# A four-tap shift convolution moved from VectorE products to TensorE matmuls with diagonal tap matrices, fed by transposing DMAs, in a kernel of two state-space layers

## The chip, the cores and the metric

The kernel runs on one core of one Trainium2 chip. The metric is the device time of one execution in microseconds. Three runs of the kernel before gave 431.73 us in the median, from 428.91 to 433.8. The profile is of one execution, with a span of 431.1 us from the first to the last instruction.

## The reference, cut to what matters

Two layers are computed side by side and their outputs are joined along the last axis. Layer A (S = 2048 rows, D = 1024 channels) starts with the four-tap convolution that the change is about, multiplies by v, applies a long convolution over the whole sequence by means of Fourier transforms, and multiplies by q:

```python
k_pad = jnp.pad(k, ((0, 0), (ks - 1, 0), (0, 0)))
k_shift = jnp.zeros_like(k)
for t in range(ks):                       # ks = 4
    k_shift = k_shift + k_pad[:, t:t + S, :] * shift_k[:, ks - 1 - t][None, None, :]
kv = k_shift * v
...
y = irfft(rfft(kv, padded to 2S) * rfft(ssm_k, padded to 2S))[:S]
y = y + kv * ssm_D
return q * y
```

Layer B is a diagonal complex recurrence: `Bu = x @ B_bar^T`, `h = Lam_bar * h + Bu[t]` along the 2048 rows, `y = 2 * real(h @ C^T) + x * Dskip`. Inputs and output are bf16.

## The kernel before, in words

The sequence of layer A is written as row = 16 n1 + n2, with n1 from 0 to 127 on the partitions and n2 from 0 to 15 as a loop. One tile is thus 128 rows, 16 apart, by 1024 channels. The Fourier transform is factored along this split, in three stages with DRAM scratch between them:

- A1. For each n2: the shift convolution and the product with v give kv (`a1_kv_ops`, L397 to L418), two 128-point transforms by matmul with F1t go to PSUM and are evicted by ScalarE (`a1_kv_mm`, L427 and L428) and stored to Ys_kv. Beside it, ssm_k is loaded in quarters (`a1h_load`), transposed on TensorE (`a1h_T`, L451), transformed (`a1h_mm`, L474) and stored to Ys_h.
- A2. For each of 32 groups g: second transforms of both (L508), the product of the spectra (L519, L521 on VectorE) and the first inverse transform (L532, L533), stored to Vs.
- A3. For each n2: the last inverse transform (L562, L563) and the product with q.

Layer B runs all the way beside these in 16 chunks of 128 rows: u = x @ B_bar^T (`b_u`, L274, 128 matmuls of 128 columns a chunk), rotation and scans on VectorE (`b_rot_ops`, L292 to L331; the scans are L305 and L308), and the output matmuls (`b_y`, L345 and L350). A prologue prepares tables and transposes B (`bt_prep`, L596 to L605); C is loaded and transposed (`ct_prep`, L618) during A1.

In the kernel before, one step n2 of the convolution uses four row tiles of k, krows[n2] to krows[n2-3]. Since neighbouring rows lie in neighbouring n2, a tap is another tile, not another partition; only for n2 < 3 is a tile needed that is shifted by one partition, with zero in the first row (`a1_load_k`, L380 to L389, with two loads for it). The taps, one per channel, are broadcast over all partitions as wbc (L374 to L378: a broadcast DMA, then two ScalarE copies). VectorE then makes four products and three sums (L406, L409, L410) and the product with v (L414), each 128x1024 in bf16.

The order of the work comes from two places. The kernel sorts closures into ticks: `at(t, kind, fn)` puts one under a tick, and each tick is issued as misc work, then TensorE work of B and A interleaved, then VectorE work of B and A interleaved. One chunk of B takes eight ticks, one n2 of A1 two (`A1_STEP`), A1 ending near tick 34. The Tile framework then orders the instructions of each engine at build time and sets semaphores; every engine and every DMA queue works its list in order. Loads go out on the queue of SP (`dma`, L85), stores on that of GpSimd (`dmas_`, L88). A tile pool with bufs = n makes the tile n allocations later wait until the earlier one is released. The pools that matter here: psa (PSUM, 3 buffers, shared by all matmuls of A), krow (6), vt (3), acc (2), hk (2 buffers of a full quarter, two times 128x2048), bn (3, for loads of B and C), and u and xT, whose depths follow U_BUFS = 5 (L245, L246). `u_tick` (L638 to L665) spreads the work of `b_u` over the ticks, at 1.5 units a tick until tick 40 and 0.7 after, no further ahead than U_BUFS chunks allow.

Of the kernel before, what the change touches and what calls it, by code (L numbers as in the profile page):

```python
# [13 lines left out]
ALU = mybir.AluOpType  # L14
F32 = mybir.dt.float32
BF16 = mybir.dt.bfloat16
# [4 lines left out]
N1, N2, NFFT = 256, 16, 4096  # L21
# [40 lines left out]
def full_kernel(ctx, tc, A_q, A_k, A_v, A_shift_k, A_ssm_k, A_ssm_D, B_x, B_Lre, B_Lim, B_Bre, B_Bim,  # L62
                B_Cre, B_Cim, B_log_dt, B_Dskip, out, cfg=None):
    cfg = dict(cfg or {})
    nc = tc.nc
    P = 128
    S, D = A_q.shape[-2], A_q.shape[-1]
# [3 lines left out]
    ND = D // P  # L71
# [3 lines left out]
    NH = D // 512  # L75
# [8 lines left out]
    def dma(out_, in_):  # L84
        return nc.sync.dma_start(out_, in_)  # L85
# [9 lines left out]
    ps_a = ctx.enter_context(tc.tile_pool(name="ps_a", bufs=3, space=PSUM))  # L95

    ident = const.tile([P, P], BF16, name="ident")
# [144 lines left out]
    hpool = ctx.enter_context(tc.tile_pool(name="b_h", bufs=2))  # L242
    ypool = ctx.enter_context(tc.tile_pool(name="b_y", bufs=2))
    state = {}
    U_BUFS = cfg.get("u_bufs", 5)  # L245
    XT_BUFS = U_BUFS + 2  # L246

    def b_load_x(i):
# [16 lines left out]
    def b_u(i, j, c):  # L265
        xT = state[("xT", i)]
        if j == 0 and c == 0:
            state[("u", i)] = upool.tile([P, 2, NJ, T], BF16, name="u", bufs=U_BUFS)
        jl = j % 2
# [94 lines left out]
    pools = {}  # L364
    kr = k.rearrange("(n s) d -> n s d", s=N2)
# [3 lines left out]
    krows = {}  # L369
    A1 = {}  # L370

    def a1_setup():
        a1 = pools["a1"]
        A1["wbc"] = a1.tile([P, 4, D], BF16, name="wbc", bufs=1)  # L374
        wraw = a1.tile([P, 2, S], BF16, name="hk", bufs=2)
        for hf in range(2):
            nc.gpsimd.dma_start(wraw[:, hf, :], A_shift_k[hf * (D // 2):(hf + 1) * (D // 2), :].rearrange("d j -> (d j)").partition_broadcast(P))
            nc.scalar.copy(A1["wbc"][:, :, hf * (D // 2):(hf + 1) * (D // 2)], wraw[:, hf, :].rearrange("p (d j) -> p j d", j=4))  # L378

    def a1_load_k(n2):  # L380
        a1 = pools["a1"]
        t_ = a1.tile([P, D], BF16, name="krow", bufs=6)
        if n2 >= 0:
            dma(t_[:], kr[:, n2, :])
        else:
            nc.gpsimd.memset(t_[0:1, :], 0.0)
            dma(t_[1:113, :], kr[0:112, N2 + n2, :])
            dma(t_[113:P, :], kr[112:P - 1, N2 + n2, :])
        krows[n2] = t_  # L389

    def a1_load_v(n2):
        a1 = pools["a1"]
        vt = a1.tile([P, D], BF16, name="vt", bufs=3)
        dma(vt[:], vr_[:, n2, :])
        A1[("vt", n2)] = vt

    def a1_kv_ops(n2):  # L397
        ops = []
        st = {}
        wbc = A1["wbc"]  # L400

        def o0():
            a1 = pools["a1"]
            st["acc"] = a1.tile([P, D], BF16, name="acc", bufs=2)
            st["m"] = a1.tile([P, D], BF16, name="m", bufs=1)
            nc.vector.tensor_mul(st["acc"][:], krows[n2 - 3][:], wbc[:, 3, :])  # L406
        ops.append(o0)
        for jj in (2, 1, 0):
            ops.append(lambda jj=jj: nc.vector.tensor_mul(st["m"][:], krows[n2 - jj][:], wbc[:, jj, :]))  # L409
            ops.append(lambda: nc.vector.tensor_add(st["acc"][:], st["acc"][:], st["m"][:]))  # L410

        def o7():
            vt = A1.pop(("vt", n2))
            nc.vector.tensor_mul(st["acc"][:], st["acc"][:], vt[:])  # L414
            A1[("kv", n2)] = st["acc"]
            krows.pop(n2 - 3)
        ops.append(o7)
        return ops  # L418

    def a1_kv_mm(n2, c, dh):  # L420
        a1 = pools["a1"]
# [12 lines left out]

    def a1h_load(qd):
        a1 = pools["a1"]
        hk = a1.tile([P, 2, S], BF16, name="hk", bufs=2)
        for t_ in range(2):
            dma(hk[:, t_, :], A_ssm_k[(2 * qd + t_) * P:(2 * qd + t_ + 1) * P, :])
        A1[("hk", qd)] = hk  # L440

    def a1h_T(qd, n2g, eng):
        a1 = pools["a1"]
        hk = A1[("hk", qd)]
        hkv = hk[:].rearrange("p t (n s) -> p t s n", s=N2)
        hT = a1.tile([P, 4, DQ], BF16, name="hT", bufs=2)
        A1[("hT", qd, n2g)] = hT
        pt = ps_t.tile([P, 4, 2, P], BF16, name="pt")
        for n2l in range(4):
            for t_ in range(2):  # L450
                nc.tensor.transpose(pt[:, n2l, t_, :], hkv[:, t_, 4 * n2g + n2l, :], ident[:])  # L451
        dst = hT[:, :, :]
        src = pt[:].rearrange("p a b c -> p a (b c)")
        if eng == "v":
            nc.vector.tensor_copy(dst, src)
        else:
            nc.scalar.copy(dst, src)
        if n2g == 0:
            dsd = a1.tile([1, DQ], BF16, name="dsd", bufs=1)
            nc.gpsimd.dma_start(dsd[:], A_ssm_D.rearrange("(o d) -> o d", o=1)[:, qd * DQ:(qd + 1) * DQ])  # L460
            nc.vector.tensor_add(hT[0:1, 0, :], hT[0:1, 0, :], dsd[:])
        if n2g == 3:
            A1.pop(("hk", qd))
# [52 lines left out]
    def a2_prod(g, which):  # L516
        x16, ha, hb = gstate[g]
        if which == 0:
            nc.vector.tensor_mul(ha[:], x16[:], ha[:])  # L519
        else:  # L520
            nc.vector.tensor_mul(hb[:], x16[:], hb[:])  # L521
# [112 lines left out]
    def at(t, kind, fn):  # L634
        assert t < NT, (t, NT)
        ev.setdefault(max(t, -1), {}).setdefault(kind, []).append(fn)
# [8 lines left out]
    for t in range(8 * NCH):  # L645
        rate = U_RATE1 if t < U_T_DRAIN else U_RATE2
        quota += rate
        while n_done < 8 * NCH:
            i_, j_ = divmod(n_done, 8)
            must = n_done < t + 8 + 2  # L650
            buf_ok = (i_ - U_BUFS) * 8 + 8 <= t - 1
            if i_ - U_BUFS < 0:
                buf_ok = True
# [40 lines left out]
    if DO_A:  # L694
        a1_last = 0
        for n2 in range(N2):
            b = A1_T0 + int(n2 * A1_STEP)
            if n2 >= 1:
                at(b - 4, "misc", lambda n2=n2: (a1_load_k(n2), a1_load_v(n2)))
            kvops = {}  # L700
            at(b, "misc", lambda n2=n2, kvops=kvops: kvops.update({"l": a1_kv_ops(n2)}))
            for oi in range(8):
                at(b + (0 if oi < 4 else 1), "dve_a", lambda oi=oi, kvops=kvops: kvops["l"][oi]())
            for bi_, (c, dh) in enumerate([(0, 0), (0, 1), (1, 0), (1, 1)]):
                at(b + 2 + bi_ // 2, "pe_a", lambda n2=n2, c=c, dh=dh: a1_kv_mm(n2, c, dh))
            a1_last = max(a1_last, b + 3)
        for qd in range(NQ):
            for n2g in range(4):
                b = A1H_T0 + (4 * qd + n2g) * A1H_STEP
                if n2g == 0 and qd + 1 < NQ:  # L710
                    at(b, "misc", lambda qd=qd: a1h_load(qd + 1))
                at(b, "pe_a", lambda qd=qd, n2g=n2g: a1h_T(qd, n2g, "s"))
                for n2l in range(4):
                    at(b + 1 + n2l // 2, "pe_a", lambda qd=qd, n2=4 * n2g + n2l: a1h_mm(qd, n2))
                a1_last = max(a1_last, b + 2)
        A2_T0 = cfg.get("a2_t0", a1_last + 6)
        assert A2_T0 - 4 > a1_last

        def switch_a2():
            cms["a1"].__exit__(None, None, None)  # L720
            cms["a2"] = tc.tile_pool(name="a2", bufs=2)
            pools["a2"] = cms["a2"].__enter__()
            a2_load(0)
            a2_load(1)
        at(A2_T0 - 4, "misc", switch_a2)
        a2_last = 0
        for g in range(NG):
            b = A2_T0 + g * A2_STEP
            if g % GC == 0 and g // GC + 2 < NG // GC:
                at(b, "misc", lambda g=g: a2_load(g // GC + 2))  # L730
            for bi_, (src, dh) in enumerate([(0, 0), (0, 1), (1, 0), (1, 1)]):
                at(b + bi_ // 2, "pe_a", lambda g=g, src=src, dh=dh: a2_s2(g, src, dh))
            at(b + 3, "dve_a", lambda g=g: a2_prod(g, 0))
            at(b + 3, "dve_a", lambda g=g: a2_prod(g, 1))
            for dh in range(NH):
                at(b + 5, "pe_a", lambda g=g, dh=dh: a2_sa(g, dh))
            a2_last = max(a2_last, b + 5)
        A3_T0 = cfg.get("a3_t0", a2_last + 8)

        def switch_a3():  # L740
            cms["a2"].__exit__(None, None, None)
            cms["a3"] = tc.tile_pool(name="a3", bufs=2)
            pools["a3"] = cms["a3"].__enter__()
        at(a2_last + 1, "misc", switch_a3)
        for n2 in range(N2):
            b = A3_T0 + int(n2 * A3_STEP)
            at(max(b - 6, a2_last + 2), "misc", lambda n2=n2: a3_load(n2))
            for dh in range(NH):
                at(b, "pe_a", lambda n2=n2, dh=dh: a3_mm(n2, dh))
            at(b + 2, "dve_a", lambda n2=n2: a3_fin(n2))  # L750
# [94 lines left out]
```

## Time and profile before

| what | value |
|---|---|
| median of three runs | 431.73 us (428.91 to 433.8) |
| span of the profiled execution | 431.1 us |
| TensorE busy | 380.7 us (88%), 3713 matmuls |
| VectorE busy | 350.7 us (81%), 642 instructions |
| ScalarE busy | 303.6 us (70%), 531 instructions |
| GpSimd busy | 130.2 us (30%) |
| DMA | 102.23 MB, mean 237 GB/s |
| mean granted TensorE clock | 0.974 |
| convolution on VectorE (L406, L409, L410, L414) | 10.9 + 32.4 + 32.3 + 10.8 us |
| tap copies on ScalarE (L378) | 4.1 us |
| loads of k | 22 DMAs, 4.6 us to landing for the full ones |

How to read it: the busy time of an engine is the union of its instructions; matmuls are pipelined, so that one of 222 ns may start every 56 ns. The page cuts the span into 40 slices of 10.8 us and gives the busy share of each engine in tenths. A row of the list of groups names the line, the engine, the operation, output<-inputs, shapes and the count; then the busy time, the mean duration of one in ns, and the idle time of the engine just before it with what ended it. A row of the waits names who waited for whom, the total, how often, and the longest. PEld is TensorE's weight load; its time overlaps the matmuls.

### The profile page before, as it was taken

How to read it: one execution, taken by the hardware profiler on the slowest of the kernel's cores; microseconds unless marked ns; L12 is line 12 of the kernel's file. 1: busy time of each engine (PE TensorE's matmuls, PEld its weight loads, DVE VectorE, ACT ScalarE, POOL GpSimd, SP SyncE). 2: the span in 40 equal slices, each digit the busy share in tenths (PEclk: the TensorE clock that was granted, in tenths of full speed). 3: DMA queues.
4: the chain of work that ended last, by engine and by line, in shares of the span. 5: the costliest groups of instructions: out<-in, count | busy, mean ns of one | idle time of the engine just before them, and what ended most of it. 6: DMA issues, size and time to landing. Idle time of an engine off the chain costs nothing.

```text
span 431.1 us, 9757 instructions
## 1 busy us (share of the span) xinstructions
PE 380.7 (88%) x3713; PEld 259.7 (60%) x3713; DVE 350.7 (81%) x642; ACT 303.6 (70%) x531; POOL 130.2 (30%) x224
## 2 busy tenths in 40 slices
PE   2589799797987997999899999999899999997784
PEld 2578687575765875775556566566465666763331
DVE  2989999999999999936897979797959637976830
ACT  1977999787886887646678877878568783344451
POOL 4000344464654455311222232322122211012121
PEclk9979999999999899999999999999899999999989
DMA  7879987778776544397778687879666523959981
GB/s 247 285 255 309 336 289 254 265 240 249 276 235 205 167 163 159 120 334 238 229 241 263 217 247 245 265 234 295 195 217 181 165 69 135 298 176 396 403 316 73
DMA packets 41353, 102.23 MB, mean 237 GB/s; under 512 B 6621, under 2 KB 8925, under 8 KB 41306
## 3 DMA queue, kind: packets, MB, share of 16 engines
q1 hardware_dynamic: 27322, 58.60, 42.7%
q0 software_dynamic: 13984, 43.01, 28.8%
q8 instruction: 29, 0.48, 0.5%
q14 instruction: 18, 0.15, 0.1%
HBM read 59.64 MB, written 33.55 MB: 216 GB/s over the span
## 4 chain that ended last, share of the span: by engine, by line
PE 42%; DVE 28%; issue 12%; DMA 10%; ACT 5%; POOL 2%; SPq 0%; POOLq 0%; DVEq 0%; ACTq 0%
PE pu L274 13%; PE py L345 13%; DVE m L409 5%; PE psa L508 5%; DVE acc L410 4%; DMA hb<-ha 3%; PE psa L533 3%; PE psa L532 3%; DVE ta L305 2%; DVE tb L308 2%; DVE acc L414 2%; DMA out_dram<-ot 2%; POOL out_dram L88 2%; DMA bn<-in_B_C_re_dram 1%; PE pt L601 1%
## 5 line engine op out<-in xcount | busy, mean ns | idle before, releaser
L274 PE MATMUL pu<-xT,BT 128*128 128x128 bf16 x2048 | 156.1, 222 | 0.5 <-ACT xT L263 0.3
L274 PEld LDWEIGHTS <-BT 128*128 128x128 bf16 x2048 | 136.2, 100 | 33.5 <-issue 2.4
L345 PE MATMUL py<-CT,h 128*128 128x512 bf16 x512 | 140.2, 382 | 2.3 <-ACT yo L355 2.3
L345 PEld LDWEIGHTS <-h 128*128 128x128 bf16 x512 | 46.7, 98 | 45.5 <-issue 4.9
L88 POOL DMA_DIRECT2D hb<-ha x64 | 33.4, 526 | 88.9 <-ACT ha L509 85.0
L534 ACT CAST vsb<-psa 128x512 bf16<-128x512 f32 x64 | 37.0, 602 | 25.7 <-PE psa L533 24.8
L88 POOL DMA_DIRECT2D Ys_h<-ysbh x64 | 45.6, 716 | 30.8 <-ACT ysbh L475 29.4
L277 ACT CAST u<-pu 128x512 bf16<-128x512 f32 x64 | 39.4, 615 | 13.2 <-PE pu L274 13.1
L428 ACT CAST ysb<-psa 128x512 bf16<-128x512 f32 x64 | 38.5, 644 | 13.7 <-PE psa L427 13.3
L519 DVE TENSOR_TENSOR ha<-x,ha 128x1024 bf16<-128x1024 bf16 x32 | 21.9, 684 | 27.8 <-DMA hb<-ha 18.7
L475 ACT CAST ysbh<-psa 128x512 bf16<-128x512 f32 x64 | 38.7, 641 | 5.5 <-issue 2.3
L509 ACT CAST ha<-psa 128x512 bf16<-128x512 f32 x64 | 36.8, 598 | 7.3 <-PE psa L508 6.3
L509 ACT CAST x<-psa 128x512 bf16<-128x512 f32 x64 | 36.9, 593 | 7.3 <-PE psa L508 5.2
L308 DVE TENSOR_TENSOR_SCAN tb<-rtab,tb 128x1024 bf16<-128x1024 f32 x16 | 36.6, 2285 | 0.0
L305 DVE TENSOR_TENSOR_SCAN ta<-rtab,ta 128x1024 bf16<-128x1024 f32 x16 | 36.5, 2280 | 0.0
L427 PE MATMUL psa<-acc,F1t 128*128 128x512 bf16 x64 | 24.6, 392 | 12.0 <-DVE acc L414 11.9
L564 ACT CAST ot<-psa 128x512 bf16<-128x512 f32 x32 | 17.9, 589 | 24.4 <-DMA out_dram<-ot 14.8
L409 DVE TENSOR_TENSOR m<-krow,wbc 128x1024 bf16<-128x1024 bf16 x48 | 32.4, 675 | 0.0
L410 DVE TENSOR_TENSOR acc<-acc,m 128x1024 bf16<-128x1024 bf16 x48 | 32.3, 673 | 0.0
L532 PE MATMUL psa<-ha,wts 128*128 128x512 bf16 x64 | 24.5, 384 | 4.2 <-DVE ha L519 4.0
L88 POOL DMA_DIRECT2D Ys_kv<-ysb x32 | 17.8, 557 | 33.9 <-ACT ysb L428 33.9
L350 PE MATMUL py<-Dd,xT 128*128 128x128 bf16 x128 | 28.0, 219 | 0.0
(139 smaller groups left out, 628.5 us busy)
## 6 DMA issues: line engine op xcount, KB each, us to landing
Ys_kv<-ysb POOLq DMA_DIRECT2D x32, 256.0 KB, 2.9
Ys_h<-ysbh POOLq DMA_DIRECT2D x64, 128.0 KB, 3.3
l2k<-Ys_kv SPq DMA_DIRECT2D x16, 512.0 KB, 6.0
l2h<-Ys_h SPq DMA_DIRECT2D x16, 512.0 KB, 4.2
hb<-ha POOLq DMA_DIRECT2D x64, 128.0 KB, 3.7
Vs<-vsb POOLq DMA_DIRECT2D x16, 512.0 KB, 5.9
vv<-Vs SPq DMA_DIRECT2D x32, 256.0 KB, 6.6
xn<-in_B_x_dram SPq DMA_DIRECT2D x16, 256.0 KB, 4.3
```

Of the source, the lines that this page charges most:

```text
L88: return nc.gpsimd.dma_start(out_, in_)
L274: nc.tensor.matmul(pu[:, c, jl, :], BT[:, j, c, dd, :], xT[:, dd, :], start=(dd == 0), stop=(dd == ND - 1))
L277: nc.scalar.copy(u[:, :, j - 1:j + 1, :], pu[:])
L305: ops.append(lambda: nc.vector.tensor_tensor_scan(fl(st["ta"]), fl(rtab), fl(st["ta"]), 0.0, ALU.mult, ALU.add))
L308: nc.vector.tensor_tensor_scan(fl(st["tb"]), fl(rtab), fl(st["tb"]), 0.0, ALU.mult, ALU.add)
L345: nc.tensor.matmul(py[:], h[:, c, j, :], CT[:, j, c, dh * 512:(dh + 1) * 512], start=(j == 0 and c == 0), stop=(j == NJ - 1 and c == 1))
L409: ops.append(lambda jj=jj: nc.vector.tensor_mul(st["m"][:], krows[n2 - jj][:], wbc[:, jj, :]))
L410: ops.append(lambda: nc.vector.tensor_add(st["acc"][:], st["acc"][:], st["m"][:]))
L428: nc.scalar.copy(ysb[:, dh * 512:(dh + 1) * 512], pt[:])
L475: nc.scalar.copy(ysbh[:, :, n2l, :], pt[:].rearrange("p (c d) -> p c d", c=2))
L509: nc.scalar.copy(d_[:, dh * 512:(dh + 1) * 512], pt[:])
L532: nc.tensor.matmul(pt[:], wts[:, gi, 1, :], ha[:, dh * 512:(dh + 1) * 512], start=True, stop=False)
```

## The change

The convolution is computed on TensorE. k is loaded by a transposing DMA on SP's queue, as tiles kT of channel (128 partitions, 8 blocks) by n1 (128 columns), with 16 columns of padding ahead. A tap j of a block of 128 channels is then a matmul with the 128x128 slice of kT as the stationary and a diagonal matrix dg[block, j] as the moving operand; four taps are summed in PSUM. The shift by one partition for n2 < 3 becomes a start one column earlier (KPAD - 1), with a zeroed column there, so the three last tiles (kTl) are loaded once, first, and serve n2 = 13, 14 and 15 too: 16 DMAs in place of 22. One n2 takes two PSUM tiles of 128x512 f32 from the pool psa, 16 matmuls each; VectorE multiplies each straight from PSUM by v into acc. The diagonal matrices are made once, by one VectorE product of identity and taps, 128x4096; wbc and its copies go. The tile m goes too. Two buffer depths change as well: U_BUFS from 5 to 4, and hk from two buffers of a full quarter to three of a half quarter.

```diff
-    U_BUFS = cfg.get("u_bufs", 5)
+    U_BUFS = cfg.get("u_bufs", 4)
...
     def a1_setup():
         a1 = pools["a1"]
-        A1["wbc"] = a1.tile([P, 4, D], BF16, name="wbc", bufs=1)
-        wraw = a1.tile([P, 2, S], BF16, name="hk", bufs=2)
-        for hf in range(2):
-            nc.gpsimd.dma_start(wraw[:, hf, :], A_shift_k[hf * (D // 2):(hf + 1) * (D // 2), :].rearrange("d j -> (d j)").partition_broadcast(P))
-            nc.scalar.copy(A1["wbc"][:, :, hf * (D // 2):(hf + 1) * (D // 2)], wraw[:, hf, :].rearrange("p (d j) -> p j d", j=4))
+        wsh = a1.tile([P, ND, 4], BF16, name="wsh", bufs=1)
+        with nc.allow_non_contiguous_dma(reason="taps, once"):
+            nc.gpsimd.dma_start(wsh[:], A_shift_k.rearrange("(b p) j -> p b j", p=P))
+        dg = a1.tile([P, ND, 4, P], BF16, name="dg", bufs=1)
+        nc.vector.tensor_tensor(dg[:].rearrange("p b j c -> p (b j) c"),
+                                ident[:].unsqueeze(1).to_broadcast([P, ND * 4, P]),
+                                wsh[:].rearrange("p b j -> p (b j)").unsqueeze(2).to_broadcast([P, ND * 4, P]), ALU.mult)
+        A1["dg"] = dg
+
+    KPAD = 16
 
     def a1_load_k(n2):
         a1 = pools["a1"]
-        t_ = a1.tile([P, D], BF16, name="krow", bufs=6)
-        if n2 >= 0:
-            dma(t_[:], kr[:, n2, :])
+        if n2 >= 0 and n2 + 3 >= N2:
+            return
+        last = n2 < 0
+        t_ = a1.tile([P, ND, KPAD + P], BF16, name="kTl" if last else "kT", bufs=3 if last else 6)
+        nc.sync.dma_start_transpose(t_[:, :, KPAD:], kr[:, n2 % N2, :])
+        if last:
+            nc.gpsimd.memset(t_[:, :, 0:KPAD], 0.0)
+            krows[n2 + N2] = t_
         else:
-            nc.gpsimd.memset(t_[0:1, :], 0.0)
-            dma(t_[1:113, :], kr[0:112, N2 + n2, :])
-            dma(t_[113:P, :], kr[112:P - 1, N2 + n2, :])
-        krows[n2] = t_
+            krows[n2] = t_
...
-    def a1_kv_ops(n2):
...
+    def a1_kv_taps(n2, dh):
+        pt = ps_a.tile([P, 512], F32, name="psa")
+        A1[("pk", n2, dh)] = pt
+        for bl in range(4):
+            b_ = 4 * dh + bl
+            for jj in range(4):
+                m = n2 - jj
+                o = KPAD if m >= 0 else KPAD - 1
+                nc.tensor.matmul(pt[:, bl * P:(bl + 1) * P], krows[m % N2][:, b_, o:o + P], A1["dg"][:, b_, jj, :],
+                                 start=(jj == 0), stop=(jj == 3))
+
+    def a1_kv_v(n2, dh):
+        a1 = pools["a1"]
+        if dh == 0:
+            A1[("kv", n2)] = a1.tile([P, D], BF16, name="acc", bufs=2)
+        sl = slice(dh * 512, (dh + 1) * 512)
+        nc.vector.tensor_mul(A1[("kv", n2)][:, sl], A1.pop(("pk", n2, dh))[:], A1[("vt", n2)][:, sl])
+        if dh == NH - 1:
+            A1.pop(("vt", n2))
...
     def a1h_load(qd):
         a1 = pools["a1"]
-        hk = a1.tile([P, 2, S], BF16, name="hk", bufs=2)
+        hk = []
         for t_ in range(2):
-            dma(hk[:, t_, :], A_ssm_k[(2 * qd + t_) * P:(2 * qd + t_ + 1) * P, :])
+            h_ = a1.tile([P, S], BF16, name="hk", bufs=3)
+            dma(h_[:], A_ssm_k[(2 * qd + t_) * P:(2 * qd + t_ + 1) * P, :])
+            hk.append(h_[:].rearrange("p (n s) -> p s n", s=N2))
         A1[("hk", qd)] = hk
...
-            kvops = {}
-            at(b, "misc", lambda n2=n2, kvops=kvops: kvops.update({"l": a1_kv_ops(n2)}))
-            for oi in range(8):
-                at(b + (0 if oi < 4 else 1), "dve_a", lambda oi=oi, kvops=kvops: kvops["l"][oi]())
+            for dh in range(NH):
+                at(b, "pe_a", lambda n2=n2, dh=dh: a1_kv_taps(n2, dh))
+                at(b + 1, "dve_a", lambda n2=n2, dh=dh: a1_kv_v(n2, dh))
```

More of the change, by code (lines that the diff above doesn't have):

```diff
@@ L395, in a1_load_v @@
         A1[("vt", n2)] = vt
-    def a1_kv_ops(n2):
[L398 to L418, printed above, removed]
+    def a1_kv_taps(n2, dh):
[16 more added lines that the diff above has]
+            A1.pop(("vt", n2))
     def a1_kv_mm(n2, c, dh):
@@ L443, in a1h_T @@
         a1 = pools["a1"]
-        hk = A1[("hk", qd)]
-        hkv = hk[:].rearrange("p t (n s) -> p t s n", s=N2)
+        hkv = A1[("hk", qd)]
         hT = a1.tile([P, 4, DQ], BF16, name="hT", bufs=2)
@@ L450, in a1h_T @@
             for t_ in range(2):
-                nc.tensor.transpose(pt[:, n2l, t_, :], hkv[:, t_, 4 * n2g + n2l, :], ident[:])
+                nc.tensor.transpose(pt[:, n2l, t_, :], hkv[t_][:, 4 * n2g + n2l, :], ident[:])
         dst = hT[:, :, :]
```

## The prediction

> **What bounds the kernel now.** I read the page's slices first, then the busy time by stage, then the waits inside the stage that changes, then single matmuls. The stages are cut by the view of the tile psa: the first matmul of A1 (L427) starts at 42.4, the first of A2 (L508) at 190.4, the first of A3 (L562) at 376.5; the span is 431.1.
>
> ```profile
> PE   2589799797987997999899999999899999997784
> ...
> DVE  2989999999999999936897979797959637976830
> ```
>
> Counted from 0, in slices 3 to 16 (10.8 us each) VectorE stands at 9 throughout while TensorE drops to 7 and 8 between; from slice 16 to 35 TensorE is at 9 in all but two, and VectorE mostly is not. By stage (TensorE, weight loads, VectorE, ScalarE, GpSimd, granted clock, DMA share, GB/s):
>
> ```profile
> 40.00:181.00 141.00, 124.09 (x1443) 96.88 (x1441) 139.56 (x241) 117.16 (x197) 66.58 (x102) 0.98 0.71 234
> 181.00:376.00 195.00, 189.91 (x1707) 120.07 (x1705) 151.77 (x260) 138.45 (x251) 48.03 (x90) 0.99 0.70 222
> ```
>
> A1 is bound by VectorE: 139.56 of 141.00. A2 is bound by TensorE: 189.91 of 195. So the change relieves the engine that sets A1, and loads the one that sets everything after it. The waits in 40 to 182 us say what the present bound costs TensorE:
>
> ```profile
> PEld L427 <- DVE acc L414: 14.6, 10, 3.1
> ...
> PE psa L427 <- DVE acc L414: 11.9, 10, 2.7
> ```
>
> The columns are total us, times, longest. In ten places TensorE's next matmul (and the weight load ahead of it, in the same time) stands still for the convolution's last product, 11.9 us in all. The work removed:
>
> ```profile
> L409 DVE TENSOR_TENSOR m<-krow,wbc 128x1024 bf16<-128x1024 bf16 x48 | 32.4, 675 | 0.0
> L410 DVE TENSOR_TENSOR acc<-acc,m 128x1024 bf16<-128x1024 bf16 x48 | 32.3, 673 | 0.0
> ```
>
> A busy TensorE is not TensorE at its peak, so I price its work from starts in a dense stretch of the timeline:
>
> ```profile
> 281.56 0.61 PE L274 MATMUL pu<-xT,BT 128*128 128x128 bf16 x8
> 282.01 0.38 PE L532 MATMUL psa<-ha,wts 128*128 128x512 bf16 x1
> 282.23 0.38 PE L533 MATMUL psa<-hb,wts 128*128 128x512 bf16 x1
> ```
>
> Eight 128-column matmuls, each with its own weights, take 282.01 - 281.56 = 0.45 us: 55.5 ns each, though one lasts 222. A 512-column one takes 0.216; a pair of 256-column ones (L474 at 108.17, next start 108.39) 0.22, or 0.109 each.
>
> **What the Trainium skill says.** "TensorE: Matmul & The Clock Gate", section Back-to-back issue gap, gives about 81 ns for a sustained 128-column matmul with its weight load and 56 ns for an isolated one; this trace has 55.5 in a stream, and I use that (81 would make the taps 41.5 instead of 28.4 us). "VectorE: DVE Perf Modes", section The perf-mode tier table, puts tensor_tensor at double rate for bf16 in SBUF and single rate with any PSUM operand; the bf16 rows above agree for the first (1024 elements in 0.67 us, against 1.22 for the f32 row L222). "DMA: Bandwidth & Descriptors" has in its table of limits (section Latency and other measured facts, row DMA_TRANSPOSE effective BW) 261 GB/s for a crossbar transpose; no run here shows one yet.
>
> **The change, part by part.** The matmul counts are those of the built program's TensorE order, cut at the same first matmuls.
>
> 1. VectorE, A1. Out go 16 x 8 = 128 products and sums. Their starts are 0.604 us apart (e.g. 55.00, 55.60, 56.20), so 77 us. In come 32 products of PSUM f32 by v, 128x512 each. Nearest rows: half of L222's f32 product, 0.61; ScalarE's eviction of the same tile, 0.59. I take 0.65: 21 us. VectorE in A1 falls from 139.6 to about 84 us and no longer sets it.
>
> 2. TensorE. In come 16 x 2 x 16 = 512 matmuls of 128 columns: 512 x 0.0555 = 28.4 us, 480 of them in A1 and 32 (1.8 us) ahead of it. At full clock A1's work is now 121.9 us: 1200 matmuls of 128 columns x 0.0555, 192 of 512 x 0.2155, 128 of 256 x 0.109. Over 148.0 us (42.4 to 190.4) at clock 0.98 (124.4) that leaves 23.6 idle: 11.9 for L414, 2.9 for hT, 2.0 for the loads of C, about 7 in small gaps. After: 1624 of 128 columns and the same others, 145.5 us, or 148.5 at 0.98. So even without any gap A1 would be as long as before. That is the heart of it: TensorE had 24 us of gaps there and is given 27 us of work.
>
> 3. The gaps that stay. L414's 11.9 go. About 8 us of the others stay. New ones: hk becomes three half buffers instead of two full pairs, so the second half of the next quarter's ssm_k can only start to load after the last transposes of the present quarter. The order has 6.7, 8.1 and 8.6 us of TensorE work between these and the first transposes of the next quarter; an hk load lands in 4.6 to 7.3 us (the view of the tile hk; median 6.8 for ssm_k on the page) after an issue of 0.43. So it just fits, or costs 1 to 2 us, three times: 0 to 5, I take 2. The queue of SP holds a transpose of k, vt and x behind that wait; they are wanted two steps (18 us) later, so they are covered, by less if a load is late. The taps also take psa: 10 tiles of three buffers a step instead of 8, and two of them wait for VectorE rather than ScalarE: 0 to 14, I take 2. A1 then is 148.5 + 8 + 2 + 2 = 160.5: +12.5.
>
> 4. u_bufs 4 instead of 5. Six steps of L274 move from A1 to A2 (888 to 840 there, 896 to 944 here) and one transposed x: A2's work goes from 176.9 to 180.0. A2 has no free TensorE, so it grows with it, 180.0/176.9 x 186.1 = 189.3: +3.2. A3's is 37.4 in both: 0.
>
> 5. The prologue. Out go two ScalarE copies of 2.1 us (L378, on the chain of waits at 12.41) and a 1 MB broadcast of shift_k. They stood ahead of the BT copies, but these are fed by B loads that land 4 us after an issue that waits for one of three buffers, so of 4.1 I count 2 gained. In comes dg, 4096 elements on VectorE: 2.4 us if it runs at the rate of the bf16 rows, 4.5 at L222's; it takes the place of six old products (3.6 us), so -1 to +1. wsh is 1024 runs of 8 bytes, wanted 30 us later: hidden. The taps of step 0: +1.8. Together about +1, if the transposes cost no more than loads.
>
> 6. The transposes, 16 instead of 22 loads. The landing is from 1.0 us of engine time (256 KB at the skill's 261 GB/s, an estimate) to several times that; the issue on SP from a load's 0.38 to some us. In A1 both are hidden up to a limit: the DMA engines are busy 0.71 x 148 = 105 us, so 13 transposes would have to take over (160 - 105)/13 = 4 us of all engines each. In the prologue four of them stand on SP ahead of the fourth B load and its followers. SP has from 5.3 to 10.45, when that load was issued before: 1.3 us each are free, all beyond that counts four times. Its loads also wait for the completion of the eighth before them in the order, so later B loads (issued at 15.3 to 22 before) wait for the four transposes to have landed, some 10 us after their issue. I take them as covered in the forecast.
>
> Sum against the profiled execution: 431.1 + 1 (prologue) + 12.5 (A1) + 3.2 (A2) + 0 = 447.8. The median of the runs shown, 431.73, is 0.6 above this span: 448.
>
> **Rivals.**
> - *The gaps close, not slower.* TensorE's 24 us were nearly all VectorE's doing and the order packs it to 3 us of gaps: A1 151.5 (+3.5), the prologue gains the full 4.1 less 1.8 (-2), A2 +3.2: about 436, and 432 if A2's 7 us of gaps halve too. For: VectorE had no idle time at all, and several small waits hang on it. Against: hT, C loads and pipeline fills are not VectorE's. It decides if A1 keeps under 4 us of gaps. Faster than 427 is hardly open: 145.5 at full clock, no gap, and all of the prologue's gain make 431.1 - 2.5 + 3.2 - 4 = 428.
> - *The transposes are slow.* At 3.4 us on SP each, four cost 4 x (3.4 - 1.3) = 8.4 in the prologue: 456. At 6 us of all engines each, A1 also gets 13 x (6 - 4) = 26 and lands about 475. For: the trace has no transposing DMA, and the skill's figure is one kernel's. Against: that figure, and that SP is mostly waiting. It decides from 1.3 us an issue in the prologue, 4 us an engine pass in A1.
> - *psa becomes the wait.* Two taps tiles wait through both scans of VectorE (2 x 2.2 us, L305 and L308), and the other matmuls of the step share one buffer at about 1 us each instead of 0.5: 3 to 4 us for each of four scan pairs, 14 in all: 460. For: the order puts the products by v behind scans in several steps. Against: VectorE is idle for over 40% of A1 then, so most tiles find it free.
>
> **How the numbers follow.** Forecast 448 (own range 440 to 456): 0.50. Gaps close (431 to 437): 0.18. Slow transposes (455 to 480): 0.17. psa (456 to 463): 0.12. Faster than 427: 0.03. The range 433 to 469 leaves out most of the faster end and the worst of the transposes, under 0.2. The runs before spread by 1%, which is about what this kernel's measurement can tell from no change. Slower by over 1% is the forecast, the transposes, psa, and a tail of the gaps case: 0.80; within 1%: 0.16; faster: 0.04.
>
> **What would show it.** Right: in A1 TensorE near 150 of 160 us and VectorE near 85; the wait of L427's successor for VectorE under 3 us; A2 close to 189; the tap matmuls 56 ns apart. Step 3 is wrong if waits for psa or hk exceed 5 us; step 5 if the first A1 matmul does not start within 41 to 45; step 6 if an issue of a transpose takes over 1.3 us or a B load waits for one. The forecast falls if the taps run at 81 ns (+13), or if A1 is shorter than 152.

## The result, and the profile after

The changed kernel takes 450.1 us in the median of three runs (449.32 to 453.69), against 431.73 before: a ratio of 1.0437, with a 95% interval from 1.0346 to 1.0529. It is slower by some 4%. The profiled execution has a span of 448.3 us, 17.2 more than before. The two slice rows that were shown of before now read, on the page of the changed kernel:

```profile
PE   4488798998999999998899999999979999998784
...
DVE  5688949183851761655779789898686838795830
```

VectorE's row of nines in slices 3 to 16 is gone, and TensorE stands at 8 or 9 from slice 5 to 28. In A1 the busiest engine is now TensorE. Cut at the same first matmuls (L431, L513 and L567 in the changed kernel's lines), the stages are:

| stage | before | after | difference | the prediction |
|---|---|---|---|---|
| prologue | 42.4 | 46.5 | +4.1 | +1 |
| A1 | 148.0 | 158.8 | +10.8 | +12.5 |
| A2 | 186.1 | 188.4 | +2.3 | +3.2 |
| A3 | 54.6 | 54.6 | 0 | 0 |
| span | 431.1 | 448.3 | +17.2 | +16.7 |

Busy times (columns as before: stretch, length, TensorE, weight loads, VectorE, ScalarE, GpSimd, granted clock, DMA share, GB/s). The first row is of the kernel before, the other two are of the changed kernel, nearly its A1 and A2:

```profile
42.00:190.00 148.00, 131.09 (x1529) 102.22 (x1527) 140.53 (x244) 118.75 (x200) 66.58 (x102) 0.98 0.71 232
...
42.00:190.00 148.00, 141.01 (x1865) 117.31 (x1863) 86.36 (x148) 114.75 (x192) 62.50 (x97) 1.00 0.69 204
190.00:394.00 204.00, 196.42 (x1805) 125.30 (x1803) 156.97 (x266) 141.95 (x259) 51.65 (x96) 1.00 0.68 221
```

In the same 148 us VectorE fell from 140.53 to 86.36, and TensorE rose from 131.09 to 141.01. The new work, from the page's groups:

```profile
L420 DVE TENSOR_TENSOR acc<-psa,vt 128x512 bf16<-128x512 f32 x32 | 21.9, 686 | 50.5 <-PE psa L412 50.4
...
L412 PE MATMUL psa<-dg,kT 128*128 128x128 bf16 x416 | 32.4, 219 | 0.8 <-DVE dg L378 0.5
```

In the last column the roles have changed: it is now VectorE that waits for the convolution, 50.4 us, and TensorE that hardly waits ahead of it (0.8). The mean of 219 ns is again no price; rows of TensorE's timeline give one:

```profile
60.42 0.33 PE L412 MATMUL psa<-dg,kT 128*128 128x128 bf16 x3
60.59 0.22 PE L412 MATMUL psa<-dg,kTl 128*128 128x128 bf16 x1
...
61.26 0.22 PE L412 MATMUL psa<-dg,kTl 128*128 128x128 bf16 x1
61.32 0.44 PE L274 MATMUL pu<-xT,BT 128*128 128x128 bf16 x5
```

Sixteen taps run from 60.42 to 61.32, 0.90 us or 56 ns each. The 512 of them cost 28.8 us of TensorE. TensorE's waits from 46.5 to 205.4 us, over all of A1:

```profile
PE psa L479 <- DVE acc L420: 4.1, 3, 1.5
PE psa L513 <- DMA wts<-a_c_W: 1.9, 1, 1.9
PE psa L431 <- DVE acc L420: 1.2, 4, 0.4
PE pt L623 <- DMA bn<-in_B_C_im_dram: 0.7, 1, 0.7
```

The 11.9 us behind the old last product (L414) have become 5.3 behind L420, 1.2 of them at L431 and 4.1 at L479. No transposed load and no half buffer of ssm_k stands in the list. That L479 waits for L420 is the psa rotation: a tile of taps not yet read by VectorE holds one of the three buffers.

### The profile page after: what moved, and what is told of

Its sections match the earlier page's. It is cut to its first block, busy times and chain, and to the rows that moved or that the text cites. A ratio compares the mean times of both kernels' runs of the same rounds, so it can differ in the third digit from the quotient of the medians.

```text
span 448.3 us, 10652 instructions
## 1 busy us (share of the span) xinstructions
PE 404.2 (90%) x4225; PEld 286.3 (64%) x4225; DVE 300.5 (67%) x547; ACT 300.2 (67%) x529; POOL 127.3 (28%) x223
## 2 busy tenths in 40 slices
DMA packets 55219, 100.47 MB, mean 224 GB/s; under 512 B 23153, under 2 KB 25473, under 8 KB 55169
## 4 chain that ended last, share of the span: by engine, by line
PE 49%; DVE 21%; DMA 10%; issue 9%; ACT 5%; SPq 2%; POOL 2%; POOLq 0%; DVEq 0%; ACTq 0%
PE pu L274 15%; PE py L345 14%; PE psa L513 4%; PE psa L412 4%; DVE ta L305 3%; DMA hb<-ha 3%; DVE tb L308 2%; PE psa L538 2%; PE psa L431 2%; PE psa L537 2%; DVE acc L420 2%; PE psa L479 2%; DMA bn<-in_B_B_re_dram 2%; DMA Ys_h<-ysbh 2%; POOL out_dram L88 2%
## 5 line engine op out<-in xcount | busy, mean ns | idle before, releaser
L274 PE MATMUL pu<-xT,BT 128*128 128x128 bf16 x2048 | 152.8, 221 | 0.4 <-ACT BT L610 0.2
L274 PEld LDWEIGHTS <-BT 128*128 128x128 bf16 x2048 | 133.0, 99 | 30.5 <-issue 1.4
L345 PE MATMUL py<-CT,h 128*128 128x512 bf16 x512 | 138.8, 381 | 2.9 <-ACT yo L355 1.4
L420 DVE TENSOR_TENSOR acc<-psa,vt 128x512 bf16<-128x512 f32 x32 | 21.9, 686 | 50.5 <-PE psa L412 50.4
L539 ACT CAST vsb<-psa 128x512 bf16<-128x512 f32 x64 | 36.9, 603 | 24.9 <-PE psa L538 23.0
L412 PE MATMUL psa<-dg,kT 128*128 128x128 bf16 x416 | 32.4, 219 | 0.8 <-DVE dg L378 0.5
L479 PE MATMUL psa<-hT,F1t 128*128 128x256 bf16 x128 | 23.1, 272 | 4.7 <-DVE acc L420 4.1
L412 PEld LDWEIGHTS <-kT 128*128 128x128 bf16 x416 | 26.2, 98 | 0.6 <-issue 0.4
```

The costliest lines, as they stand in the source:

```text
L274: nc.tensor.matmul(pu[:, c, jl, :], BT[:, j, c, dd, :], xT[:, dd, :], start=(dd == 0), stop=(dd == ND - 1))
L345: nc.tensor.matmul(py[:], h[:, c, j, :], CT[:, j, c, dh * 512:(dh + 1) * 512], start=(j == 0 and c == 0), stop=(j == NJ - 1 and c == 1))
L412: nc.tensor.matmul(pt[:, bl * P:(bl + 1) * P], krows[m % N2][:, b_, o:o + P], A1["dg"][:, b_, jj, :], start=(jj == 0), stop=(jj == 3))
L539: nc.scalar.copy(vsb[:, gi, dh * 512:(dh + 1) * 512], pt[:])
```

## The experiments

The kernel before ran beside each group of kernels on the same chip, 7 to 23 times. Its medians there were 431.59 (one tap, the buffers in the kernel before, plain loads), 432.82 (idle taps, one product on GpSimd, dg on GpSimd, four halves) and 430.62 (two taps, evictions, dg early). The ratios are of the runs taken side by side, and can differ a little from the quotient of two medians. Stage lengths are of one profiled execution each.

**One tap of four.** Three taps are left out of the sum, so 384 matmuls fall away and all else stays.

```diff
-            for jj in range(4):
+            for jj in range(1):
...
-                                 start=(jj == 0), stop=(jj == 3))
+                                 start=True, stop=True)
```

> The changed kernel with one tap of four: a1_kv_taps issues 4 matmuls of 128 columns a tile instead of 16 (it leaves out three taps of the convolution), all else the same: same tiles of psa, same products on VectorE, same transposes. If TensorE's work sets A1, 384 x 0.0555 = 21 us go and A1 keeps its gaps: 448 - 21 = 427, or 424 to 432 beside 450 for the changed kernel. If the passage of the tiles through psa and VectorE sets it, or the transposes do, their number is the same and the time stays at 442 to 450.

Measured: 437.35 us, ratio 1.0132 (1.0046 to 1.0218), between the two expected ranges. The 21.3 us of matmuls taken out bring back 12.8. A1 (47.1 to 194.9) is 147.8 us, as long as before, though VectorE is far from full in it:

```profile
47.00:195.00 148.00, 134.22 (x1573) 105.77 (x1587) 90.81 (x157) 117.17 (x199) 66.88 (x103) 0.98 0.69 216
```

By count its A1 holds 125.5 us of TensorE work, 3.6 more than before (1264 matmuls of 128 columns in place of 1200). VectorE is relieved of 50 us (140.53 to 90.81) and TensorE loaded with 4, and A1 is as long as before, at the same granted clock of 0.98. The waits for L414 are gone, but TensorE has others from 47.1 to 194.9:

```profile
PE psa L479 <- DVE acc L420: 4.6, 2, 2.4
PE pt L623 <- DMA bn<-in_B_C_im_dram: 2.7, 1, 2.7
PE psa L431 <- ACT ysbh L480: 1.1, 1, 1.1
```

All waits that this view names sum to 11.1 us here and to 16.7 in A1 before. Of the 5.6 us that went, the added work takes 3.6. So less than half of the 11.9 behind L414 came back as shorter waits. The kernel also has the changed buffers, so it doesn't show relief by itself. Of the 437.35 - 431.59 = 5.8 us above the kernel before, 4.7 lie in the prologue by the traces (47.1 against 42.4).

**Two taps of four.** The same edit with `range(2)`: two taps are left out.

> The changed kernel with two taps of four (256 matmuls of 128 columns instead of 512; it leaves out two taps). With one tap A1 took 148 us, as long as before, although VectorE was relieved; with four 159. If A1 has a floor near 148 that is not TensorE's, and TensorE takes over only above it (its A1 work is 132 here, plus the 13 us of gaps it had with four taps = 145): 437 to 440. If every matmul costs in proportion (21.3 us of work gave 12.7): 441 to 443.

Measured: 439.84 us, ratio 1.0218 (1.0133 to 1.0302), in the range expected of a floor. Here A1 (45.7 to 194.6) is 148.9 us, with 132.1 us of TensorE work. The second tap added 6.6 us of work and 1.1 us of length, the third and fourth 13.4 of work and 9.9 of length. But the granted clock in A1 was 1.00 here and 0.98 with one tap, which by the forecast's reckoning is 2.6 us of the one-tap kernel's work (125.5/0.98), and a one-tap kernel below that ran at 1.00 has an A1 of 145.4. Beside that one the second tap adds 3.5. So a floor near 148 is not shown. What is shown is that the last two taps cost more of their work than the second one, while the gaps shrink. The intervals of the two ratios overlap.

**Buffers, in the kernel before.** First u_bufs 4 together with hk as three half buffers, then u_bufs alone.

```diff
-    U_BUFS = cfg.get("u_bufs", 5)
+    U_BUFS = cfg.get("u_bufs", 4)
...
-        hk = a1.tile([P, 2, S], BF16, name="hk", bufs=2)
+        hk = []
...
+            h_ = a1.tile([P, S], BF16, name="hk", bufs=3)
```

> The kernel before with the two buffer changes alone: U_BUFS 4 and hk in three half buffers. The forecast's steps 3 and 4: some steps of L274 move from A1, where TensorE has gaps, to A2, where it has none (+3), and hk costs 0 to 5: +3 to +5, about 435. If the buffers are the main cost of the change, +8 or more. If they cost nothing, within 1% of before.

> The kernel before with U_BUFS 4 alone, to part the two buffer changes. Step 4 says +3 (434 to 435); if the half buffers of hk are what costs, this one stays at the time of before and e2 is slower.

Measured: 439.2 us for both together, some 4 more than expected, ratio 1.0163 (1.0086 to 1.024), and 434.36 for u_bufs alone, as expected, ratio 1.0048 (1.0019 to 1.0077). The second gives the depth of 4 a price of about 2 us in the kernel before (2.1 by the ratio, 2.8 by the medians). The first can't be read as the price of the halves: in it the broadcast of shift_k also went through the half buffers, and 3.6 of its loss lie in the prologue (A1 began at 46.0). Its A1 took 149.4 us, at a clock of 0.95, and TensorE waited 1.6 us in it for a half buffer of ssm_k; with u_bufs alone A1 took 146.7.

**Half buffers, in the changed kernel.** Here the halves get a fourth buffer; the room comes from the padding of kT where it isn't used.

```diff
-            h_ = a1.tile([P, S], BF16, name="hk", bufs=3)
+            h_ = a1.tile([P, S], BF16, name="hk", bufs=4)
```

> The changed kernel with hk in four half buffers, as much as before, paid for by leaving the 16 columns of padding out of the kT tiles that don't need it. If the half buffers cost what step 3 allows for (0 to 5 us of waits for a load of ssm_k): 446 to 450; the trace shows no wait of L456 for hk, so no gain is likelier: 449 to 451.

Measured: 451.36 us, ratio 1.0436 (1.0357 to 1.0515), the same as the changed kernel. The three halves cost nothing that can be seen.

**Plain loads for transposing ones.** Same bytes into the same tiles by a plain DMA on the same queue, so the convolution is computed of untransposed rows.

```diff
-        nc.sync.dma_start_transpose(t_[:, :, KPAD:], kr[:, n2 % N2, :])
+        dma(t_[:, :, KPAD:], kr[:, n2 % N2, :].rearrange("n (b c) -> n b c", b=ND))
```

> The changed kernel with plain loads of the same bytes in place of the 16 transposing DMAs (it leaves out the transposition, so other numbers go into the same matmuls). If the transposes are covered, only the 0.65 us by which the fourth load of B was issued later comes back, and what hangs on it: 446 to 450. If they are what holds the prologue or A1 (their issue takes 1.3 us, and many small packets share the DMA engines), 5 us or more come back: below 445.

Measured: 450.06 us, ratio 1.042 (1.0346 to 1.0494). The transposition costs this kernel nothing in the sum. By the view of their line in the changed kernel, the transposes take 1.3 us of SP each and land about as fast as the plain loads (3.0, 3.5 and 6.9 there):

```profile
L391 SPq DMA_TRANSPOSE kT<-in_A_k_dram x13: 1242/1307/2015, 9.7 to 129.2; - x13
...
DMA to landing us min/median/max: 3.4/3.8/6.6
```

Two limits of this run show in its profile. The plain loads fill the same tiles in pieces as small: 22896 packets under 512 bytes, against 23153 with transposes and 6621 before, so a cost of the small packets would be in both. And the cheaper issues did bring the loads of B forward, the fourth to 8.85 us from 11.10, the last to 30.64 from 32.75. But the last one took 6.2 us to land, TensorE waited 3.1 us for it, and A1 started at 47.8.

**TensorE's load alone.** The kernel before keeps its convolution on VectorE; TensorE gets 512 more matmuls of 128 columns at the places of the taps, and nobody reads their sums. VectorE is not relieved.

```diff
+    def a1_idle_taps(n2, dh):
+        pt = ps_a.tile([P, 512], F32, name="psa")
+        for bl in range(4):
+            b_ = 4 * dh + bl
+            for jj in range(4):
+                nc.tensor.matmul(pt[:, bl * P:(bl + 1) * P], krows[n2 - jj][:, b_ * P:(b_ + 1) * P], ident[:],
+                                 start=(jj == 0), stop=(jj == 3))
...
```

> The kernel before with 512 matmuls of 128 columns added at the ticks and into the pool that the changed kernel gives to the taps (their sums are read by nobody), and nothing taken off VectorE. It gives what TensorE's load alone costs. If TensorE's work is what lengthens A1: A1's 145.5 us at least, with VectorE's waits partly filled: 445 to 458. If the matmuls fit into the waits for VectorE: 432 to 438. The difference to the changed kernel is what relieving VectorE is worth.

Measured: 447.96 us, ratio 1.0369 (1.031 to 1.0429), in the range expected if TensorE's work lengthens A1. This is the run that decides. Its stretch from 42 to 190 us:

```profile
42.00:190.00 148.00, 140.57 (x1838) 117.33 (x1849) 138.35 (x234) 112.78 (x190) 62.41 (x96) 0.99 0.65 213
```

VectorE stands at 138.35 here and at 86.36 in the changed kernel, TensorE at 140.57 and 141.01. A1 is 161.6 us here (44.8 to 206.4) and 158.8 there; this kernel's A1 holds 148.6 us of TensorE work (121.9 + 480 x 0.0555), that one's 145.5. So 13.0 and 13.3 us of it are gaps (at clocks of 0.99 and 1.00), with a full VectorE and with one that is idle for over 40% of the time. The load on TensorE explains the loss, and the relief of VectorE brought nothing against it that can be seen. The wait for the last product, 11.9 us before, has all but gone without any relief, from 44.8 to 206.4:

```profile
PE psa L435 <- DVE acc L414: 1.5, 2, 0.8
```

With more work ahead of it in TensorE's list, L435 mostly finds the product done.

**One product on GpSimd.** In the kernel before, the first of the four products of a step goes to GpSimd: a relief of VectorE that costs TensorE nothing.

```diff
-            nc.vector.tensor_mul(st["acc"][:], krows[n2 - 3][:], wbc[:, 3, :])
+            nc.gpsimd.tensor_mul(st["acc"][:], krows[n2 - 3][:], wbc[:, 3, :])
```

> The kernel before with one of the eight products and sums of a step (L406) on GpSimd: 16 x 0.60 = 9.7 us leave VectorE, nothing is added to TensorE. If VectorE alone set A1 before: 422 to 425. If TensorE, ScalarE and the buffers stand right behind it: 428 to 432. If GpSimd's product takes over 2 us and holds the stores behind it: slower than before.

Measured: 458.59 us, ratio 1.0626 (1.0557 to 1.0695), the expected outcome for a slow product on GpSimd. It relieved nothing. The view of the line:

```profile
L406 POOL TENSOR_TENSOR acc<-krow,wbc x16: 2119/2938/4721, 16.6 to 188.5; 128x1024 bf16<-128x1024 bf16 x16
```

A product of 0.68 us on VectorE takes 2.9 on GpSimd, 4.7 at worst, and VectorE's busy time over the span rose from 350.7 to 368.2 us with 16 instructions fewer. The run shows that this is no way out; about what relief alone is worth it says nothing.

**The diagonal matrices made elsewhere.** First on GpSimd, then on VectorE in four pieces at an earlier place, near where it had waited 4.2 us for ScalarE (they ran at 8.5, 14.9, 16.6 and 18.3).

```diff
-        nc.vector.tensor_tensor(dg[:].rearrange("p b j c -> p (b j) c"),
+        nc.gpsimd.tensor_tensor(dg[:].rearrange("p b j c -> p (b j) c"),
```

> The changed kernel with the product that makes dg on GpSimd instead of VectorE. In the trace of the changed kernel it holds VectorE for 4.42 us ahead of the last copy of B (L608 at 38.38, its transposes done at 35.8), and the first rotation starts at 41.1 instead of 37.3. GpSimd is idle there. If dg's place is the prologue's loss: 2 to 3 us come back, 447 to 448. If GpSimd needs over 30 us for it, or the prologue is late for another reason: 450 or more.

```diff
     def params_rest():
...
+        cms["a1"] = tc.tile_pool(name="a1", bufs=2)
+        pools["a1"] = cms["a1"].__enter__()
+        a1_setup()
...
-        nc.vector.tensor_tensor(dg[:].rearrange("p b j c -> p (b j) c"),
+        for b_ in range(0, ND, 2):
+            nc.vector.tensor_tensor(dg[:, b_:b_ + 2].rearrange("p b j c -> p (b j) c"),
...
```

> The changed kernel with dg made in four pieces of 128x1024 at the place where VectorE waits 4.25 us for the sine of L159, instead of one of 4.42 us ahead of the last copy of B. If dg's place costs the prologue: the last copy of B comes at 36.4 instead of 38.4 and 2 to 3 us come back, 447 to 448. If the later start has other reasons: 449 to 451.

Measured: 451.21 us, ratio 1.0432 (1.0361 to 1.0502), and 454.04, ratio 1.0525 (1.0443 to 1.0606), which lies outside both of its ranges. Neither got anything back. On GpSimd the product takes 7 us by the profile, and one small product of VectorE stands still nearly as long. A row of each engine's timeline:

```profile
4.67 7.02 POOL L378 TENSOR_TENSOR dg<-ident,wsh 128x4096 bf16<-128x4096 bf16 x1 [1.13 <-DMA wsh<-in_A_shift_k_dram]
```

```profile
5.40 6.31 DVE L171 TENSOR_TENSOR den<-p 128x8 f32<-128x8 f32 x1
```

The same line takes 0.17 in the changed kernel, and the next product of this shape (L172) takes 0.15 here. The Trainium skill, "SBUF — State Buffer", section SBUF: two separate sides, describes a port pair that VectorE and GpSimd share and that one of them holds for a whole instruction while the other blocks, for a VectorE product with both inputs in SBUF too; the 6.31 us agree with that, as L171 ends when GpSimd's product does. The last loads of B are issued at 32.83 and 33.50 instead of 32.08 and 32.75, its last copy ends at 39.99 instead of 39.06, and the first L292 comes at 41.33 as against 41.13. In both kernels the order of the build changed: A1's first transform comes at 37.6 and 40.4 instead of 46.5, with 128 and 160 fewer matmuls ahead of it, so that the prologue is no longer the same work. In the second the taps of step 0 also stand early in TensorE's list, ahead of transposes of B, and wait for their k there.

```profile
13.42 0.29 PE L416 MATMUL psa<-dg,kT 128*128 128x128 bf16 x1 [2.59 <-DMA kT<-in_A_k_dram]
```

On SP's queue no load of B is issued between 21.6 and 30.5 us, where the changed kernel issues four; three loads of x, three transposes of k and others stand there. The last copy of B comes at 43.79 instead of 38.38. So neither run tells what dg's place alone costs, and that stays open.

**Evictions on VectorE.** Half of ScalarE's evictions of the first transforms go to the idle VectorE, once with one tap only (three left out), once with four taps and dg early.

```diff
-        nc.scalar.copy(ysb[:, dh * 512:(dh + 1) * 512], pt[:])
+        if c == 1:
+            nc.vector.tensor_copy(ysb[:, dh * 512:(dh + 1) * 512], pt[:])
+        else:
+            nc.scalar.copy(ysb[:, dh * 512:(dh + 1) * 512], pt[:])
```

> The changed kernel with one tap of four (three left out) and half of the evictions of L432 (c = 1, 32 of 0.64 us) on VectorE instead of ScalarE. It asks what holds A1 at 148 us there. If ScalarE (22.8 of 25.0 us busy between 75 and 100): A1 falls by up to 10, 427 to 434. If the prologue's order, the loads or the passage through psa hold it: 435 to 440.

> The changed kernel with both: dg early, and half of the evictions of L432 on VectorE, which is idle for 45% of A1. If TensorE alone sets A1 with four taps, the evictions give nothing beyond dg: 446 to 449. If part of the 9 us in which TensorE is idle in A1 are late evictions: 440 to 445. In neither case as fast as before.

Measured: 438.29 us, ratio 1.0178 (1.0109 to 1.0247), with one tap, as expected if ScalarE is not the limit; 460.44, ratio 1.0702 (1.063 to 1.0774), with four, far above both of its ranges. The two ratios of one tap lie within each other's intervals. A1 took 145.4 us in the first (46.0 to 191.4), with ScalarE busy for 101.9 instead of 117; the 2.4 us less are about what the clock is worth, 1.00 instead of 0.98. So 15 us off ScalarE gave nothing that can be told from the clock. The second is 6.4 us worse than dg early alone. TensorE's waits in 46 to 216 us of it:

```profile
PE psa L486 <- DVE acc L424: 4.5, 3, 1.8
PE psa L435 <- DVE acc L424: 3.6, 6, 0.9
...
PE psa L486 <- DVE ysb L437: 1.4, 3, 0.6
```

The same view of dg early alone has 4.3 for the first and 1.2 for the second of these, and no third. These waits are 4.0 us longer in sum: TensorE stands behind a VectorE whose list holds one more kind of work, though VectorE has time to spare. No version that was tried beats the kernel before.

## Why the prediction was right

The forecast was 448, the measured median is 450.1. The mechanism is right: TensorE's work in A1 is what makes the kernel slower, and A1 carries most of the loss. That the sum came within 0.5 us of the measured span (+16.7 against +17.2) is in part luck, because the terms miss by +3.1 in the prologue, -1.7 in A1 and -0.9 in A2. By signs that the prediction had set itself, steps 3 and 5 are wrong: waits for psa above 5 us, and a first A1 matmul outside 41 to 45. Step by step:

1. *VectorE in A1, 139.6 to 84.* Right. Measured 86.36 in the 148 us from 42, and 90.8 in all of A1. L420 takes 0.69 us against the 0.65 taken.

2. *TensorE, 145.5 us of work in A1.* Right, and it is the cause. The taps run at 56 ns, not at the 81 that the Trainium skill's "TensorE: Matmul & The Clock Gate" (Back-to-back issue gap) gives for a stream; each tap has its own weights, so the trace's 55.5 was the better price. The idle taps put this cause to the test: that load alone makes 15.1 of the 18.4 us between the medians. One condition was off: the granted clock in A1 was 1.00, not 0.98, worth about 3 us by the forecast's own reckoning (148.5 - 145.5).

3. *The gaps that stay, 12 us.* Right in sum, not in parts. At full clock the gaps are 158.8 - 145.5 = 13.3. The half buffers, priced at 2, cost nothing (run with four, and no wait in the trace). The waits for VectorE through psa, priced at 2 between 0 and 14, are 4.1 + 1.2 = 5.3. The loads of C fell from 2.0 to 0.7. And the 11.9 behind L414 shrank to 1.5 under the load alone, as the idle taps show, so they were no gain of the relief.

4. *u_bufs, +3.2 in A2.* Right in size: A2 grew by 2.3 (the forecast's own quotient gives 189.4, not 189.3), and u_bufs alone cost the kernel before 2.1 to 2.8. That it costs them in A2 is less sure: in the profiled execution of u_bufs alone A2 is 186.7, 0.6 longer than before, A1 1.3 shorter and A3 1.5 longer.

5. *The prologue, +1.* Mis-sized: +4.1. The end of it, first in the timeline of the kernel before (its last transposes and its last copy of B), then in that of the changed kernel:

```profile
33.93 0.62 PE L601 MATMUL pt<-ident,bn 128*128 128x128 bf16 x8
...
34.58 1.01 ACT L605 COPY BT<-pt 128x1024 bf16<-128x1024 bf16 x1 [0.43 <-PE pt L601]
```

```profile
34.05 4.42 DVE L378 TENSOR_TENSOR dg<-ident,wsh 128x4096 bf16<-128x4096 bf16 x1
...
35.07 1.27 PE L606 MATMUL pt<-ident,bn 128*128 128x128 bf16 x16 [0.33 <-DMA bn<-in_B_B_re_dram]
...
36.38 1.01 ACT L610 COPY BT<-pt 128x1024 bf16<-128x1024 bf16 x1 [0.76 <-PE pt L606]
...
38.38 0.68 DVE L608 COPY BT<-pt 128x1024 bf16<-128x1024 bf16 x1
...
41.13 0.69 DVE L292 TENSOR_TENSOR ta<-u,ci 128x1024 bf16<-128x1024 bf16 x1 [2.07 <-ACT u L277]
```

dg takes 4.42 us, the upper of the two bounds. That was to be had from the Trainium skill: "VectorE: DVE Perf Modes", section What auto-detection actually checks, wants a step of 1 or -1 in every tensor for the double rate, and the taps are broadcast with step 0; 4096 elements in 4.42 us agree with the single rate, as L222's f32 row did (1024 in 1.22). It was counted as standing in for six old products of 3.6 us, but it stands as one block ahead of the last copy of B. Those products had come one by one between the copies. The last transposes of B end at 36.34 and the last copy at 39.06; before these were 34.55 and 35.59. Of these 3.5 us, 1.8 lie ahead of the transposes, with loads of B that came later (the last two were issued at 32.08 and 32.75 instead of 30.57 and 31.24), and 1.7 between transposes and copy, where dg stands. The two ScalarE copies that went gave nothing back that can be seen. This split is only read from the trace. The idle taps have neither dg nor transposing loads, and still end B's last transposes at 36.97 and start A1 at 44.8, 2.4 us later than before. So over half of the 4.1 may belong to the taps on TensorE, which step 5 had at 1.8. In the run with plain loads dg is over at 35.5, before the last transposes of B start at 36.9, and A1 starts no earlier. What dg's place costs stays open; with dg in this place the start of A1 also scatters, from 45.7 to 47.8 in six kernels.

6. *The transposes, covered.* Right in the sum. An issue takes 1.31 us in the median where 1.3 were free, and up to 2.0; the fourth load of B went out at 11.10 instead of 10.45; plain loads in their place do not change the time. Whether the many small packets cost anything no run shows, as the plain loads have them too.

The rivals: slow transposes, by their issue or their landing, are refuted by the plain loads and by the landing times. psa as a wait is there, at 5.3 us of the 14. That the gaps close was the closest rival, and the runs say why it failed. TensorE's work and the length of A1, from one execution of each kernel (the work counted in the built program and priced at full clock):

| kernel | VectorE in 148 us | TensorE work in A1 | A1 | gaps | granted clock in A1 |
|---|---|---|---|---|---|
| before | 140.5 | 121.9 | 148.0 | 26.1 | 0.98 |
| one tap | 90.8 | 125.5 | 147.8 | 22.3 | 0.98 |
| two taps | 91.1 (of 149) | 132.1 | 148.9 | 16.8 | 1.00 |
| before, idle taps | 138.4 | 148.6 | 161.6 | 13.0 | 0.99 |
| changed | 86.4 | 145.5 | 158.8 | 13.3 | 1.00 |

The gaps shrink as work is added, and with the most work they are 13, whether VectorE is full or not. So the sentence "A1 is bound by VectorE" was too strong. VectorE was busy 139.56 of 141 us, but with 50 us of that taken off and TensorE nearly as before, A1 kept its 148: other waits took the place of the one for L414. The stretch of 141 us also ends 9.4 us before A1 does. In these 9.4 us TensorE is busy without a break and VectorE for 3.0. Nor is the passage to A2 a wait of A1 before: 14.6 us go by from the last first transform to A2 (175.8 to 190.4), with a store and a load in between, and TensorE fills them all with other work; after the change it waits 1.9 us there. ScalarE is not it either. What relief of VectorE alone, with nothing else changed, would have been worth stays open, as the one run for it, the product on GpSimd, didn't relieve it. Of the 13.3 us of gaps that remain, the view of the waits names 8.5; the rest was not taken apart.

## What to carry to other kernels

Add up the work that each engine would hold in the stage, not only the waits that go: here the engine that was to take the work had 26 us of gaps, was given 24, and half of the gaps stayed. A busy share near 100% doesn't prove that an engine sets a stage: take its work away in a run of its own, and put the new load on the other engine in another, before counting on the relief. A wait that can be read in a trace is not yet time to be won: 11.9 us of waiting for a product shrank to 1.5 when TensorE got more to do, and gave place to other waits when the product got cheaper. And look at what stands behind a block of several us on one engine's list: here a copy whose input was there at 36.34 started at 38.38, behind dg. Whether small pieces would have been cheaper no run shows.

## What the runs showed of the hardware

- A transposing DMA of 128x1024 bf16 lands in 3.8 us in the median (3.4 to 6.6), a plain one into the same tiles in 3.5 (3.0 to 6.9); its issue on SP takes 1.31 us in the median, a plain one 0.38.
- The packets of under 512 bytes rose from 6621 to 23153 with the change. With plain loads into the same tiles there were 22896, so what they cost was not measured.
- While GpSimd ran a 7.02 us product, a 128x8 product on VectorE took 6.31 us instead of 0.17. GpSimd took 2.1 to 4.7 us for a bf16 product of 128x1024 that takes VectorE 0.68.
- A bf16 product of 128x4096 on VectorE with one operand broadcast along its row took 4.42 us, and in four pieces of 128x1024 1.21 us each; a plain bf16 product of 128x1024 took 0.67.
- A stream of 128-column matmuls, each with its own 128x128 weights, runs at 56 ns a matmul at a granted clock of 1.00.
